# A SwiGLU block: one Silu with a token-major down projection, and gate and val as two 64-row array tiles

## The chip, the cores and the metric

The kernel runs on one core of a Trainium2 chip. The metric is the device time of one execution in microseconds (us), lower is better. PE is TensorE's matrix multiplication, PEld its weight loads, DVE is VectorE, ACT is ScalarE, POOL is GpSimd, SP is SyncE, which here only starts DMAs. "Granted clock" is the share of TensorE's full clock that the hardware let through (1.00 is full).

## The reference, cut to what matters

A depthwise causal convolution with 7 taps runs over the sequence (x is 8 x 4096 x 192, one softmaxed set of taps for each of 8 heads of 24 channels). A gated feed-forward block follows on all 32768 tokens:

```python
g   = x @ w_gate                 # 192 -> 1536
val = x @ w_val                  # 192 -> 1536
out = (g * sigmoid(g) * val) @ w_out     # 1536 -> 192
```

## The kernel before

The tokens are cut into 64 blocks of 512. For a block, x is fetched, transposed on PE so that channels lie on partitions (two halves of 96), and convolved. Taps are shared out: ACT makes the first product and the products for POOL, DVE adds 3 or 4 taps, POOL adds the last 2 or 3. The 1536 hidden features are 12 chunks of 128. This happens for each chunk:

```python
def emit_chunk(j, xcb, hlist):
    gps = ppool.tile([P, TB], fp32, tag="gate", name="gate")   # two buffers each
    for h in range(2):
        nc.tensor.matmul(gps, wg_r[:, h, ts(j, P)], xcb[h], start=(h == 0), stop=(h == 1))
    vps = ppool.tile([P, TB], fp32, tag="val", name="val")
    for h in range(2):
        nc.tensor.matmul(vps, wv_r[:, h, ts(j, P)], xcb[h], start=(h == 0), stop=(h == 1))
    nc.scalar.activation(sj, gps, AF.Sigmoid)
    nc.vector.tensor_tensor(qj, gps, sj, op=ALU.mult)          # q = gate * sigmoid
    if j in A_CHUNKS:                                          # 4 of 12
        nc.vector.tensor_tensor(hj, qj, vps, op=ALU.mult)
    else:                                                      # 8 of 12
        nc.scalar.copy(v_sb, vps)
        nc.gpsimd.tensor_tensor(hj, qj, v_sb, op=ALU.mult)

def emit_f2(j, acc, hlist):              # down projection, features on partitions
    for m in range(2):
        nc.tensor.matmul(acc[:, m, :], wo_r[:, j, m * Dh : (m + 1) * Dh], hlist[j], ...)

def emit_store(b, acc):
    nc.vector.transpose(outB, acc)       # 96 x 1024, back to token rows in 32 x 32 squares
    ...                                  # six DMAs of 128-byte runs
```

The conv of the next block is emitted among the chunks of this one:

```python
for k in DVE_TAPS[h]:
    nc.vector.scalar_tensor_tensor(out=xacc, in0=xcin[:, k : k + TB],
        scalar=wsm[h][:, k : k + 1], in1=xacc, op0=ALU.mult, op1=ALU.add)
... # ACT makes tmp for each k in POOL_TAPS[h]
for i, tmp in enumerate(tmps):           # POOL adds them; the last add gives xc_h
    nc.gpsimd.tensor_tensor(o, xacc, tmp, op=ALU.add)
```

## Time and profile before

| | before |
|---|---|
| time, median of 2 runs | 1695.25 us (1694.97 to 1695.53) |
| a block of 512 tokens, span / 64 | 26.5 us |
| busy share PE, DVE, ACT, POOL | 77, 72, 61, 64% |
| mean granted clock | 0.876 |

Parts 1, 2 and 4 of the page of the kernel before (busy us, share of the span and instructions; the granted clock in tenths, over 40 slices; the chain of waits that ended last):

```profile
PE 1304.3 (77%) x5120; PEld 605.6 (36%) x5120; DVE 1229.0 (72%) x1547; ACT 1040.1 (61%) x1861; POOL 1080.7 (64%) x967
...
PEclk9898888888898898888988888889889889898899
...
POOL 26%; PE 24%; DVE 23%; issue 15%; ACT 9%; POOLq 0%; DVEq 0%; ACTq 0%
```

No engine is full and the chain hops over all of them: the kernel is bound by a loop of hand-overs, not by one engine. Part 5 of the page, the groups of instructions (line, engine, operation, out<-in, shapes, count, then busy us, mean ns of one, then the engine's idle time before them and what ended most of it):

```profile
L185 POOL TENSOR_TENSOR h<-q,vsb 128x512 f16<-128x512 f16 x512 | 624.1, 1225 | 436.6 <-DVE q L178 303.9
L190 PE MATMUL acc<-h,wo_sb 128*96 128x512 f16 x1536 | 503.5, 412 | 322.0 <-POOL h L185 316.9
L178 DVE TENSOR_TENSOR q<-gate,sig 128x512 f16<-128x512 f32 x768 | 513.1, 681 | 189.6 <-ACT sig L176 127.5
L145 DVE SCALAR_TENSOR_TENSOR xacc<-xcin,wn_98,xacc 96x512 f32<-96x512 f16 x256 | 273.5, 1068 | 107.5 <-ACT xacc L143 106.9
L145 DVE SCALAR_TENSOR_TENSOR xacc<-xcin,wn_111,xacc 96x512 f32<-96x512 f16 x192 | 261.6, 1362 | 2.0 <-ACT xacc L143 1.6
L201 DVE STREAM_TRANSPOSE outB<-acc 96x1024 f32<-96x1024 f32 x64 | 79.7, 1245 | 140.3 <-PE acc L190 140.1
```

The POOL product is the slow step of the loop: 1.2 us each, and PE waits 317 us for it. The taps (L145) have two means, 1.07 and 1.36 us, for one shape; the shortest are 0.73 us. Every longer one ran beside POOL: the 42 taps (of 448) during which POOL ran no sum or product took 0.73 to 0.75 us each. Here is POOL in the timeline of the kernel before, at the end of a block (start us, us, engine, line, operation):

```profile
818.82 1.26 POOL L161 TENSOR_TENSOR xc<-xacc,tmp_6_7455 96x512 f16<-96x512 f32 x1
820.04 1.15 POOL L185 TENSOR_TENSOR h<-q,vsb 128x512 f16<-128x512 f16 x1
821.15 1.71 POOL L161 TENSOR_TENSOR xc<-xacc,tmp_6_7518 96x512 f16<-96x512 f32 x1
822.83 1.15 POOL L185 TENSOR_TENSOR h<-q,vsb 128x512 f16<-128x512 f16 x1
```

Conv sums and h products share one queue, so an h that PE waits for stands behind sums that nobody yet needs.

### The profile page before, as it was taken

The numbers are of one execution on the slowest core, as the hardware profiler recorded it, in microseconds if no ns is written. First come the engines' busy times: TensorE is split into PE (matmuls) and PEld (weight loads), VectorE is DVE, ScalarE is ACT, GpSimd is POOL, SyncE is SP. The second block draws the span as 40 slices with busy tenths as digits, with TensorE's granted clock in tenths as the row PEclk, the third lists the DMA queues.
The fourth block names the chain that finished last, engine by engine and source line by source line (L and its number), as shares of the span: only waits on it lengthen the run. The fifth ranks groups of instructions, "written<-read, shape, count | busy, mean of one in ns | idle before, by whom it ended". The sixth has DMA issues, their size and how long they took to land.

```text
span 1696.6 us, 18246 instructions
## 1 busy us (share of the span) xinstructions
PE 1304.3 (77%) x5120; PEld 605.6 (36%) x5120; DVE 1229.0 (72%) x1547; ACT 1040.1 (61%) x1861; POOL 1080.7 (64%) x967
## 2 busy tenths in 40 slices
PE   3777777878787787787787877877877878778777
PEld 1333333333333333343333333433333333334333
DVE  5787677777686786776776867777777768677765
ACT  4766656656566666576666665656666656666545
POOL 4777666576666666766666667567566666675664
PEclk9898888888898898888988888889889889898899
DMA  5111102111111111021110111110211101111101
GB/s 139 29 38 28 38 10 47 35 22 38 19 38 29 28 38 38 10 47 30 27 38 19 38 29 28 38 29 19 47 27 30 38 19 38 28 29 19 18 11 28
DMA packets 238813, 55.06 MB, mean 32 GB/s; under 512 B 204024, under 2 KB 238328, under 8 KB 238712
## 3 DMA queue, kind: packets, MB, share of 16 engines
q1 hardware_dynamic: 238712, 53.90, 15.3%
q8 instruction: 40, 0.66, 0.2%
q14 instruction: 61, 0.50, 0.1%
HBM read 28.71 MB, written 25.17 MB: 32 GB/s over the span
## 4 chain that ended last, share of the span: by engine, by line
POOL 26%; PE 24%; DVE 23%; issue 15%; ACT 9%; POOLq 0%; DVEq 0%; ACTq 0%
POOL h L185 13%; DVE q L178 11%; POOL xc L161 10%; PE gate L167 9%; DVE xacc L145 9%; PE val L172 6%; PE acc L190 6%; ACT sig L176 5%; POOL xacc L161 4%; DVE h L181 3%; ACT vsb L184 2%; ACT xacc L143 0%; ACT xcin L140 0%; DVE outB L201 0%; POOLq L185 0%
## 5 line engine op out<-in xcount | busy, mean ns | idle before, releaser
L185 POOL TENSOR_TENSOR h<-q,vsb 128x512 f16<-128x512 f16 x512 | 624.1, 1225 | 436.6 <-DVE q L178 303.9
L190 PE MATMUL acc<-h,wo_sb 128*96 128x512 f16 x1536 | 503.5, 412 | 322.0 <-POOL h L185 316.9
L176 ACT ACTIVATE sig<-gate 128x512 f16<-128x512 f32 x768 | 456.7, 595 | 476.0 <-PE gate L167 440.7
L178 DVE TENSOR_TENSOR q<-gate,sig 128x512 f16<-128x512 f32 x768 | 513.1, 681 | 189.6 <-ACT sig L176 127.5
L167 PE MATMUL gate<-xc,wg_sb 96*128 96x512 f16 x1536 | 515.6, 420 | 40.6 <-DVE q L178 32.7
L172 PE MATMUL val<-xc,wv_sb 96*128 96x512 f16 x1536 | 537.0, 422 | 1.3 <-ACT vsb L184 0.5
L190 PEld LDWEIGHTS <-wo_sb 128*96 128x96 f16 x1536 | 199.4, 130 | 537.3 <-issue 414.5
L145 DVE SCALAR_TENSOR_TENSOR xacc<-xcin,wn_98,xacc 96x512 f32<-96x512 f16 x256 | 273.5, 1068 | 107.5 <-ACT xacc L143 106.9
L184 ACT CAST vsb<-val 128x512 f16<-128x512 f32 x512 | 297.6, 581 | 39.5 <-PE val L172 38.9
L145 DVE SCALAR_TENSOR_TENSOR xacc<-xcin,wn_111,xacc 96x512 f32<-96x512 f16 x192 | 261.6, 1362 | 2.0 <-ACT xacc L143 1.6
L167 PEld LDWEIGHTS <-wg_sb 96*128 96x128 f16 x1536 | 161.3, 105 | 253.8 <-issue 135.5
L172 PEld LDWEIGHTS <-wv_sb 96*128 96x128 f16 x1536 | 162.5, 106 | 207.0 <-issue 70.1
L201 DVE STREAM_TRANSPOSE outB<-acc 96x1024 f32<-96x1024 f32 x64 | 79.7, 1245 | 140.3 <-PE acc L190 140.1
L181 DVE TENSOR_TENSOR h<-q,val 128x512 f16<-128x512 f16 x256 | 171.8, 671 | 7.9 <-PE val L172 1.2
L143 ACT ACTIVATE xacc<-xcin,wn_98 96x512 f32<-96x512 f16 x64 | 46.2, 722 | 75.4 <-POOL xc L161 75.3
L143 ACT ACTIVATE xacc<-xcin,wn_111 96x512 f32<-96x512 f16 x64 | 46.0, 719 | 34.9 <-POOL xc L161 34.9
L138 POOL COPY xcin<-xcin 96x6 f16<-96x6 f16 x112 | 37.5, 335 | 37.4 <-ACT xcin L140 37.4
L126 PE MATMUL xt_129<-identity,x_sb 128*96 128x128 f32 x4 | 1.1, 421 | 19.9 <-DMA x_sb<-in_x_dram 19.9
L109 POOL CAST wo_sb<-wo_st 128x2304 f16<-128x2304 f32 x1 | 2.1, 2104 | 17.4 <-DMA wo_st<-in_moe_w_out_dram 17.4
L104 DVE CAST wv_sb<-wv_st 96x3072 f16<-96x3072 f32 x1 | 1.8, 1757 | 9.0 <-DMA wv_st<-in_moe_w_val_dram 9.0
L126 PEld LDWEIGHTS xt_129<-identity,x_sb 128*96 128x96 f32 x4 | 0.6, 190 | 19.9 <-issue 19.9
L99 ACT CAST wg_sb<-wg_st 96x3072 f16<-96x3072 f32 x1 | 2.8, 2751 | 4.7 <-DMA wg_st<-in_moe_w_gate_dram 4.7
(1043 smaller groups left out, 963.2 us busy)
## 6 DMA issues: line engine op xcount, KB each, us to landing
x_sb<-in_x_dram SPq DMA_DIRECT2D x64, 384.0 KB, 3.4
out_dram<-outB SPq DMA_DIRECT2D x384, 64.0 KB, 1.9
wg_st<-in_moe_w_gate_dram SPq DMA_DIRECT2D x1, 1152.0 KB, 8.5
wv_st<-in_moe_w_val_dram SPq DMA_DIRECT2D x1, 1152.0 KB, 13.1
wo_st<-in_moe_w_out_dram SPq DMA_DIRECT2D x1, 1152.0 KB, 15.3
wraw_87<-in_weight_dram SPq DMA_DIRECT2D x1, 2.6 KB
wraw_100<-in_weight_dram SPq DMA_DIRECT2D x1, 2.6 KB
```

The costliest lines, as they stand in the source:

```text
L143: nc.scalar.mul(xacc, xcin[:, 0:TB], wsm[h][:, 0:1])
L145: nc.vector.scalar_tensor_tensor(out=xacc, in0=xcin[:, k : k + TB], scalar=wsm[h][:, k : k + 1], in1=xacc, op0=ALU.mult, op1=ALU.add,)
L161: nc.gpsimd.tensor_tensor(o, xacc, tmp, op=ALU.add)
L167: nc.tensor.matmul(gps, wg_r[:, h, ts(j, P)], xcb[h], start=(h == 0), stop=(h == 1))
L172: nc.tensor.matmul(vps, wv_r[:, h, ts(j, P)], xcb[h], start=(h == 0), stop=(h == 1))
L176: nc.scalar.activation(sj, gps, AF.Sigmoid)
L178: nc.vector.tensor_tensor(qj, gps, sj, op=ALU.mult)
L181: nc.vector.tensor_tensor(hj, qj, vps, op=ALU.mult)
L184: nc.scalar.copy(v_sb, vps)
L185: nc.gpsimd.tensor_tensor(hj, qj, v_sb, op=ALU.mult)
L190: nc.tensor.matmul(acc[:, m, :], wo_r[:, j, m * Dh : (m + 1) * Dh], hlist[j], start=(j == 0), stop=(j == NCH - 1),)
L201: nc.vector.transpose(outB, acc)
```

## The change

The intent is threefold. Silu in one ACT instruction removes q, the val copy and POOL's products, so that DVE makes h with one product per chunk. The down projection becomes token-major: h is the stationary operand, so the result comes out with tokens on partitions, and the transpose and small stores go. And gate and val, whose 192 input channels had been two 96-row matmuls each, become three slots of 64 channels: gate on array rows 0 to 63 and val on rows 64 to 127 are meant to run at the same time, so that 4 matmul times become 3. For this the conv result is copied by 8 on-chip DMAs a block into both row ranges. The core of the diff (weight loading, pool lines and signatures cut):

```diff
+    def emit_slots(xcs):
+        xq = cpool.tile([P, NQ, TB], fp16, tag="xq", name="xq")
+        for lo in (0, Q):
+            ...          # 4 copies for each row range, all on the SP queue
+                nc.sync.dma_start(out=xq[r : r + n, c // Q, :],
+                                  in_=xcs[c // Dh][c % Dh : c % Dh + n, :])
+        return xq
     def emit_chunk(j, xcb, hlist):
-        ...              # two gate matmuls, two val matmuls, 96 rows each
+        for q in range(NQ):
+            for lo, ps in ((0, gps), (Q, vps)):
+                nc.tensor.matmul(ps, w_r[lo : lo + Q, q, ts(j, P)],
+                    xcb[lo : lo + Q, q, :], start=(q == 0), stop=(q == NQ - 1))
-        nc.scalar.activation(sj, gps, AF.Sigmoid)
-        nc.vector.tensor_tensor(qj, gps, sj, op=ALU.mult)
-        ...              # h on DVE (4 chunks), or val copy on ACT and h on POOL (8)
+        nc.scalar.activation(sj, gps, AF.Silu)
+        nc.vector.tensor_tensor(hj, sj, vps, op=ALU.mult)
     def emit_f2(j, acc, hlist):
-        for m in range(2):
-            nc.tensor.matmul(acc[:, m, :], wo_r[:, j, m * Dh : (m + 1) * Dh], hlist[j], ...)
+        for s in range(SUBS):
+            nc.tensor.matmul(acc[s // 2][:, s % 2, :], hlist[j][:, ts(s, P)], wo_r[:, j, :], ...)
     def emit_store(b, acc):
-        nc.vector.transpose(outB, acc)       # and six stores
+        nc.scalar.copy(o_sb[:, 0:2, :], acc[0])
+        nc.vector.tensor_copy(o_sb[:, 2:4, :], acc[1])   # and one store
-                if j == 5: ...  elif j == 8: ...     # conv halves of the next block
+                if j == 1: ...  elif j == 4: ...
```

More of the change, by code (lines that the diff above doesn't have):

```diff
@@ L53 @@
     POOL_TAPS = {0: (5, 6), 1: (4, 5, 6)}
-    A_CHUNKS = frozenset((0, 3, 6, 9))
     F2_LAG = 2
+    Q = 64
+    NQ = D // Q
     const_pool = ctx.enter_context(tc.tile_pool(name="const", bufs=1))
@@ L94 @@
         wsm.append(wn)
-    wg_st = wpool.tile([Dh, 2, Dff], fp32, tag="wg_st", name="wg_st")
-    nc.sync.dma_start(out=wg_st, in_=moe_w_gate.rearrange("(h p) f -> p h f", p=Dh))
-    wg_r = wpool.tile([Dh, 2, Dff], fp16, tag="wg_sb", name="wg_sb")
-    nc.scalar.copy(wg_r, wg_st)
-    wv_st = wpool.tile([Dh, 2, Dff], fp32, tag="wv_st", name="wv_st")
-    nc.sync.dma_start(out=wv_st, in_=moe_w_val.rearrange("(h p) f -> p h f", p=Dh))
-    wv_r = wpool.tile([Dh, 2, Dff], fp16, tag="wv_sb", name="wv_sb")
-    nc.vector.tensor_copy(wv_r, wv_st)
+    w_st = wpool.tile([P, NQ, Dff], fp32, tag="w_st", name="w_st")
+    nc.sync.dma_start(out=w_st[0:Q], in_=moe_w_gate.rearrange("(q p) f -> p q f", p=Q))
+    nc.sync.dma_start(out=w_st[Q:P], in_=moe_w_val.rearrange("(q p) f -> p q f", p=Q))
+    w_r = wpool.tile([P, NQ, Dff], fp16, tag="w_sb", name="w_sb")
+    nc.scalar.copy(w_r[:, 0, :], w_st[:, 0, :])
+    nc.vector.tensor_copy(w_r[:, 1, :], w_st[:, 1, :])
+    nc.gpsimd.tensor_copy(w_r[:, 2, :], w_st[:, 2, :])
     wo_st = wpool.tile([P, NCH, D], fp32, tag="wo_st", name="wo_st")
@@ L162, in emit_conv_half @@
         return xc_h
+    def emit_slots(xcs):
+        xq = cpool.tile([P, NQ, TB], fp16, tag="xq", name="xq")
+        for lo in (0, Q):
+            c = 0
+            while c < D:
+                n = min(Q - c % Q, Dh - c % Dh)
+                r = lo + c % Q
+                nc.sync.dma_start(
+                    out=xq[r : r + n, c // Q, :],
+                    in_=xcs[c // Dh][c % Dh : c % Dh + n, :],
+                )
+                c += n
+        return xq
     def emit_chunk(j, xcb, hlist):
@@ L165, in emit_chunk @@
         gps = ppool.tile([P, TB], fp32, tag="gate", name="gate")
-        for h in range(2):
-            nc.tensor.matmul(
-                gps, wg_r[:, h, ts(j, P)], xcb[h], start=(h == 0), stop=(h == 1)
-            )
         vps = ppool.tile([P, TB], fp32, tag="val", name="val")
-        for h in range(2):
-            nc.tensor.matmul(
-                vps, wv_r[:, h, ts(j, P)], xcb[h], start=(h == 0), stop=(h == 1)
-            )
-        sj = hpool.tile([P, TB], fp16, tag="sig", name="sig")
@@ L176, in emit_chunk @@
-        nc.scalar.activation(sj, gps, AF.Sigmoid)
-        qj = hpool.tile([P, TB], fp16, tag="q", name="q")
-        nc.vector.tensor_tensor(qj, gps, sj, op=ALU.mult)
-        hj = hpool.tile([P, TB], fp16, tag="h", name="h", bufs=4)
-        if j in A_CHUNKS:
-            nc.vector.tensor_tensor(hj, qj, vps, op=ALU.mult)
-        else:
-            v_sb = hpool.tile([P, TB], fp16, tag="vsb", name="vsb")
-            nc.scalar.copy(v_sb, vps)
-            nc.gpsimd.tensor_tensor(hj, qj, v_sb, op=ALU.mult)
+        for q in range(NQ):
+            for lo, ps in ((0, gps), (Q, vps)):
+                nc.tensor.matmul(
+                    ps,
+                    w_r[lo : lo + Q, q, ts(j, P)],
+                    xcb[lo : lo + Q, q, :],
+                    start=(q == 0),
+                    stop=(q == NQ - 1),
+                )
@@ L186, in emit_chunk @@
+        sj = hpool.tile([P, TB], fp16, tag="sig", name="sig", bufs=3)
+        nc.scalar.activation(sj, gps, AF.Silu)
+        hj = hpool.tile([P, TB], fp16, tag="h", name="h", bufs=5)
+        nc.vector.tensor_tensor(hj, sj, vps, op=ALU.mult)
         hlist.append(hj)
     def emit_f2(j, acc, hlist):
-        for m in range(2):
+        for s in range(SUBS):
             nc.tensor.matmul(
-                acc[:, m, :],
-                wo_r[:, j, m * Dh : (m + 1) * Dh],
-                hlist[j],
-                start=(j == 0),
+                acc[s // 2][:, s % 2, :],
+                hlist[j][:, ts(s, P)],
+                wo_r[:, j, :],
+                start=(j == 0 and s % 2 == 0),
@@ L195, in emit_f2 @@
                 stop=(j == NCH - 1),
+                skip_group_check=True,
             )
@@ L199, in emit_store @@
         t0 = b * TB
-        outB = opool.tile([Dh, 2, TB], fp32, tag="outB", name="outB")
-        nc.vector.transpose(outB, acc)
-        for m in range(2):
-            for a in range(Dh // 32):
-                dst = bass.AP(
-                    tensor=out.tensor,
-                    offset=t0 * D + m * Dh + 32 * a,
-                    ap=[[D, 32], [32 * D, TB // 32], [1, 32]],
-                )
-                nc.sync.dma_start(out=dst, in_=outB[ts(a, 32), m, :])
+        o_sb = opool.tile([P, SUBS, D], fp32, tag="o_sb", name="o_sb")
+        nc.scalar.copy(o_sb[:, 0:2, :], acc[0])
+        nc.vector.tensor_copy(o_sb[:, 2:4, :], acc[1])
+        nc.sync.dma_start(
+            out=out[t0 : t0 + TB, :].rearrange("(s p) d -> p s d", p=P), in_=o_sb
+        )
     x_sb_next = emit_fetch(0)
@@ L219 @@
         if p == 0:
-            xc_blk[0] = [emit_conv_half(0, h, xts[h]) for h in range(2)]
+            xc_blk[0] = emit_slots([emit_conv_half(0, h, xts[h]) for h in range(2)])
             continue
         b = p - 1
-        acc = apool.tile([Dh, 2, TB], fp32, tag="acc", name="acc")
+        acc = [
+            apool.tile([P, 2, D], fp32, tag=f"acc{i}", name=f"acc{i}") for i in range(2)
+        ]
         hlist = []
@@ L229 @@
             if p < n_blocks:
-                if j == 5:
-                    xc_blk[p] = [emit_conv_half(p, 0, xts[0]), None]
-                elif j == 8:
-                    xc_blk[p][1] = emit_conv_half(p, 1, xts[1])
+                if j == 1:
+                    xc0 = emit_conv_half(p, 0, xts[0])
+                elif j == 4:
+                    xc_blk[p] = emit_slots([xc0, emit_conv_half(p, 1, xts[1])])
         for j in range(NCH - F2_LAG, NCH):
```

## The prediction

> **What bounds it now.** 64 blocks of 512 tokens, about 26.3 us each (span 1696.6 us). No engine is full: the busy table gives PE 77%, DVE 72%, POOL 64%, ACT 61%; the chain that ended last is shared by POOL 26%, PE 24%, DVE 23%, issue 15%. It is a coupled pipeline: matmul, sigmoid, q on DVE, ScalarE copy of val, product on POOL (1225 ns x512), down matmul. Largest waits: sigmoid for gate matmul (440.7 us), down matmul for POOL's h (316.9), POOL's h for q (303.9). In the timeline, from 804 to 817 us the clock is 1.00 and DVE 99% busy; from 817 to 829 us PE waits for POOL (conv sums queue ahead of h) and the clock falls to 0.75.
>
> **What changes, per block (groups' means, timeline).**
> - DVE: 12 q products (0.68 us) go; all 12 h products become SBUF sig x PSUM val, a form that cost 0.67 us. The 1.25 us transpose becomes a half copy[...]. The 7 conv taps stay: 0.65 to 0.74 us alone, up to 2.29 beside POOL (means 1.07, 1.36).[...] About 19 -> 14 us.
> - POOL: 8 h products (9.8 us) go: about 17 -> 7 us, so fewer slow taps.
> - ACT: 8 val copies (0.47 us start to start) go, a half copy comes: about 16 -> 13 us. Silu est. like sigmoid, 0.595.
> - PE: gate+val were 4 matmuls of 0.215 us a chunk; now 3 pairs, 0.65 us if they overlap fully.[...] Down: 2x0.215 becomes 4 matmuls of 192 columns with a new weight load each[...].[...]
> - DMA: 8 on-chip copies; 6 -> 1 stores, in 768 B runs. Est. 2 us to land (old stores: 1.9). With conv emitted at chunks 1 and 4, they land 2 to 3 us before use.
>
> **Critical path after.** The built kernel's queues show two phases a block. A (first 4 or 5 chunks): conv work interleaves with Silu and h; I count 12.7 us from the last block's final gate/val pairs to the fifth h, set by DVE (7 taps, two waiting for POOL's sums) behind the accumulator drain. B (the rest): paced by PE or by the two-buffer loop pair, Silu, product (2.2 us per 2 chunks): 6 x 1.1 to 1.25 us. Sum 19.5 to 20.3 us a block; x64 plus some 25 us start: about 1275 us, 25% less.
>
> **Predicted:** 1275 us, 8 in 10 in 1140 to 1430. Faster by over 2%: 0.95; within 2%: 0.03; slower: 0.02.
>
> **What would show it.**
> - A pair's matmuls start within tens of ns, three pairs take 0.65 us; if not, 1.29.
> - [...]
> - Taps' mean about 0.9 us; POOL 30 to 35% busy, DVE 70%, ACT 65%.
> - Waits: PE for DVE's h at the front of a block; none long for xq DMAs.
> - Clock above 0.9, as PE no longer waits for POOL.
>
> **What would make it wrong.** Pairs serialised: about 24 us a block, 1560.[...] xq landing late: PE stalls and goes cold at block starts, +2 to 4 us. Opposite: phases overlapping better, 17.5 us a block, 1145.

What is cut from it came from no trace of this case, or was an estimate that does not say from what it was made. Its sums came to about 14 us a block on DVE, and to 19.5 to 20.3 us a block on the path (the two phases as written add up to 12.7 + 6.6 to 7.5, that is 19.3 to 20.2), so about 1275 us. Terms of both are cut: the half copy that takes the transpose's place on DVE (measured later: 0.56 us), and what a chunk costs on TensorE with four down matmuls and two changes between 64-row and 128-row matmuls (measured later: 1.19 us). The lower 1.1 us a chunk of phase B is half of the loop's 2.2 us; the upper 1.25 us can't be derived from what is left.

## More of the kernel before

The program order is not the order on the engines: a scheduler builds each engine's queue from readiness and order of emission.

## The result, and the profile after

| | before | after |
|---|---|---|
| time, median | 1695.25 us | 1361.55 us (1361.24 to 1361.87, 2 runs) |
| ratio to before | 1 | 0.803 (95% interval 0.801 to 0.806) |
| a block, span / 64 | 26.5 us | 21.2 us |
| busy share PE, DVE, ACT, POOL | 77, 72, 61, 64% | 84, 70, 59, 35% |
| mean granted clock | 0.876 | 0.919 |

A ratio, here and below, is the mean time of one kernel's fast runs over that of the other's of the same rounds, so it is not quite the ratio of the medians quoted.

Parts 1, 2, 4 and 5 of the page after, to be held against those of before:

```profile
PE 1142.1 (84%) x8192; PEld 498.6 (37%) x8192; DVE 953.4 (70%) x1291; ACT 798.3 (59%) x1413; POOL 478.9 (35%) x456
...
PEclk9999898998998889989989889889899899888899
...
PE 48%; DVE 29%; issue 15%; ACT 7%; DMA 1%; SPq 0%; ACTq 0%; DVEq 0%
...
L185 PE MATMUL val<-xq,w_sb 64*128 64x512 f16 x2304 | 684.5, 412 | 153.0 <-DVE h L195 152.6
L195 DVE TENSOR_TENSOR h<-sig,val 128x512 f16<-128x512 f16 x768 | 523.8, 682 | 314.1 <-ACT sig L193 311.4
L146 DVE SCALAR_TENSOR_TENSOR xacc<-xcin,wn_111,xacc 96x512 f32<-96x512 f16 x192 | 238.2, 1241 | 2.7 <-ACT xacc L144 0.4
L146 DVE SCALAR_TENSOR_TENSOR xacc<-xcin,wn_98,xacc 96x512 f32<-96x512 f16 x256 | 196.4, 767 | 32.3 <-ACT xacc L144 29.9
```

POOL has left the chain. Half 0's taps (wn_98) fell from 1068 to 767 ns, but half 1's (wn_111) are still at 1241, and PE waits 153 us for DVE's h. The timeline of the kernel after, in one block, shows where these two meet:

```profile
805.44 1.26 POOL L162 TENSOR_TENSOR xacc<-xacc,tmp_5_9589 96x512 f32<-96x512 f32 x1 [1.30 <-DVE xacc L146]
805.88 3.05 DVE L146 SCALAR_TENSOR_TENSOR xacc<-xcin,wn_111,xacc 96x512 f32<-96x512 f16 x2
806.78 1.59 POOL L162 TENSOR_TENSOR xc<-xacc,tmp_6_9591 96x512 f16<-96x512 f32 x1
808.85 0.67 DVE L195 TENSOR_TENSOR h<-sig,val 128x512 f16<-128x512 f16 x1
809.58 0.37 PE L185 MATMUL val<-xq,w_sb 64*128 64x512 f16 x1 [2.01 <-DVE h L195]
```

Two half-1 taps are queued in front of the fourth h. They meet half 0's two sums on POOL and take 3.05 us, where the two taps at the start of the same block take 1.53. The first tap begins while the first sum runs (to 806.70), and the pair of taps ends at 808.93, 0.56 us after the second sum (808.37); a tap alone takes 0.75 us. The whole trace agrees: the 311 taps (of 448) beside which no sum ran took 0.73 to 0.75 us each, the other 137 took 1.49 us on average. Why the hardware makes a tap beside a sum longer, no run shows. Meanwhile PE sits idle for 2.01 us, since val has two buffers and the fourth h holds one. The same block by windows (stretch in us, its length, busy us and count for PE, PEld, DVE, ACT, POOL, then granted clock, DMA share, GB/s):

```profile
800.60:807.40 6.80, 6.05 (x45) 2.53 (x44) 6.32 (x10) 6.80 (x14) 2.56 (x4) 1.00 0.42 116
807.40:809.58 2.18, 0.17 (x2) 0.00 (x1) 2.18 (x3) 0.43 (x1) 0.97 (x1) 1.00 0.01 1
809.58:811.10 1.52, 1.52 (x9) 0.63 (x8) 1.45 (x3) 0.60 (x1) 0.77 (x1) 0.71 0.37 94
811.10:813.60 2.50, 2.50 (x13) 0.84 (x14) 0.80 (x2) 0.60 (x1) 2.38 (x4) 0.50 0.10 27
813.60:820.40 6.80, 6.60 (x58) 3.07 (x54) 3.76 (x6) 3.15 (x6) 0.67 (x1) 1.00 0.11 29
```

Soon after the gap the clock falls to half for 3.41 us (810.21 to 813.62 in the trace's clock records), so the loss is the gap and then slow chunks, which follow each other after 1.53, 2.15 and 1.35 us. The chunks after those run at full clock, 1.19 us each. The whole trace repeats this: it has 60 waits of about 2.0 us, and at 59 of them the clock falls to half within 1.6 us of the wait's end.

### The profile page after: what moved, and what is told of

It reads as the page before. It is cut to its first block, busy times and chain, and to the rows that moved or that the text cites. A ratio compares the mean times of both kernels' runs of the same rounds, so it can differ in the third digit from the quotient of the medians.

```text
span 1359.5 us, 22727 instructions
## 1 busy us (share of the span) xinstructions
PE 1142.1 (84%) x8192; PEld 498.6 (37%) x8192; DVE 953.4 (70%) x1291; ACT 798.3 (59%) x1413; POOL 478.9 (35%) x456
## 4 chain that ended last, share of the span: by engine, by line
PE 48%; DVE 29%; issue 15%; ACT 7%; DMA 1%; SPq 0%; ACTq 0%; DVEq 0%
PE gate L185 25%; DVE xacc L146 18%; DVE h L195 11%; PE val L185 6%; ACT xacc L144 3%; ACT sig L193 3%; DMA x_sb<-in_x_dram 1%; ACT o_sb L213 0%; PE acc_446 L201 0%; PE acc_699 L201 0%; PE acc_16118 L201 0%; PE acc_11325 L201 0%; PE acc_14361 L201 0%; PE acc_8289 L201 0%; PE acc_5253 L201 0%
## 5 line engine op out<-in xcount | busy, mean ns | idle before, releaser
L185 PE MATMUL val<-xq,w_sb 64*128 64x512 f16 x2304 | 684.5, 412 | 153.0 <-DVE h L195 152.6
L195 DVE TENSOR_TENSOR h<-sig,val 128x512 f16<-128x512 f16 x768 | 523.8, 682 | 314.1 <-ACT sig L193 311.4
L185 PE MATMUL gate<-xq,w_sb 64*128 64x512 f16 x2304 | 701.2, 410 | 25.0 <-ACT sig L193 17.3
L185 PEld LDWEIGHTS <-w_sb 64*128 64x128 f16 x4608 | 211.8, 97 | 483.9 <-issue 391.2
L201 PEld LDWEIGHTS <-h 128*128 128x128 f16 x3072 | 232.1, 102 | 347.9 <-issue 315.9
L146 DVE SCALAR_TENSOR_TENSOR xacc<-xcin,wn_111,xacc 96x512 f32<-96x512 f16 x192 | 238.2, 1241 | 2.7 <-ACT xacc L144 0.4
L139 POOL COPY xcin<-xcin 96x6 f16<-96x6 f16 x112 | 46.1, 411 | 531.7 <-ACT xcin L141 531.7
L146 DVE SCALAR_TENSOR_TENSOR xacc<-xcin,wn_98,xacc 96x512 f32<-96x512 f16 x256 | 196.4, 767 | 32.3 <-ACT xacc L144 29.9
L127 PE MATMUL xt_128<-identity,x_sb 128*96 128x128 f32 x4 | 1.1, 417 | 20.3 <-DMA x_sb<-in_x_dram 20.3
L127 PEld LDWEIGHTS xt_128<-identity,x_sb 128*96 128x96 f32 x4 | 0.6, 187 | 20.3 <-issue 20.2
L162 POOL TENSOR_TENSOR xacc<-xacc,tmp_5_5794 96x512 f32<-96x512 f32 x1 | 1.3, 1263 | 12.0 <-DVE xacc L146 12.0
L162 POOL TENSOR_TENSOR xacc<-xacc,tmp_5_11866 96x512 f32<-96x512 f32 x1 | 1.3, 1263 | 12.0 <-DVE xacc L146 12.0
L162 POOL TENSOR_TENSOR xacc<-xacc,tmp_5_1746 96x512 f32<-96x512 f32 x1 | 1.3, 1265 | 11.9 <-DVE xacc L146 11.9
L162 POOL TENSOR_TENSOR xacc<-xacc,tmp_5_13890 96x512 f32<-96x512 f32 x1 | 1.3, 1263 | 11.9 <-DVE xacc L146 11.9
L162 POOL TENSOR_TENSOR xacc<-xacc,tmp_5_7818 96x512 f32<-96x512 f32 x1 | 1.3, 1263 | 11.9 <-DVE xacc L146 11.9
L162 POOL TENSOR_TENSOR xacc<-xacc,tmp_5_15912 96x512 f32<-96x512 f32 x1 | 1.3, 1267 | 11.8 <-DVE xacc L146 11.8
## 6 DMA issues: line engine op xcount, KB each, us to landing
wo_st<-in_moe_w_out_dram SPq DMA_DIRECT2D x1, 1152.0 KB, 15.2
```

The lines of the kernel that those rows point to most:

```text
L127: nc.tensor.transpose(xt[:, ts(s, P)], x_sb[:, s, h * Dh : (h + 1) * Dh], identity)
L139: nc.gpsimd.tensor_copy(xcin[:, 0:pad], prev_xcin[h][:, TB : TB + pad])
L185: nc.tensor.matmul(ps, w_r[lo : lo + Q, q, ts(j, P)], xcb[lo : lo + Q, q, :], start=(q == 0), stop=(q == NQ - 1),)
L195: nc.vector.tensor_tensor(hj, sj, vps, op=ALU.mult)
L201: nc.tensor.matmul(acc[s // 2][:, s % 2, :], hlist[j][:, ts(s, P)], wo_r[:, j, :], start=(j == 0 and s % 2 == 0), stop=(j == NCH - 1), ski ...
```

## The experiments

Twelve kernels ran, three rounds each, on chips where the kernel before took 1694 to 1695 us. All gave the right result except the one that was wrong on purpose. The theory after reading the two traces was: work taken off DVE and POOL gave the gain; the tiles gave little; a collision of taps with POOL sums, and the clock after it, held the rest back. The rivals were that TensorE's new form carries the gain, and that DVE's sum of work paces the block whatever its order.

### One part undone at a time

**a_half96: row tiles and on-chip copies undone, the rest kept.**

```diff
-        for q in range(NQ):
-            for lo, ps in ((0, gps), (Q, vps)):
-                nc.tensor.matmul(ps, w_r[lo : lo + Q, q, ts(j, P)], ...)
+        for w, ps in ((wg_r, gps), (wv_r, vps)):
+            for h in range(2):
+                nc.tensor.matmul(ps, w[:, h, ts(j, P)], xcb[h], ...)
```

> Changed kernel with only the row tiles and the on-chip copies undone: gate and val as four 96-row matmuls from the two conv halves, as before. Theory (row tiling is worth little here): a chunk on TensorE costs 4 x 0.215 + 0.35 us = 1.21 us without the two gaps of about 0.09 us at mode changes, against 1.19 us measured with tiles; so 1361 us within 30 us. Rival (the pairs are the gain): +0.215 us per chunk on the path, 12 x 64 x 0.215 = +165 us, about 1525 us.

Measured: 1090.95 us, ratio 0.644 (0.643 to 0.645), clock 0.993. Both expectations missed: it is 20% faster than the whole change. The TensorE part of the theory held, though. PE in the timeline of a_half96, one chunk when nothing holds it up:

```profile
705.49 0.60 PE L176 MATMUL gate<-xc,wg_sb 96*128 96x512 f16 x2
705.92 0.59 PE L176 MATMUL val<-xc,wv_sb 96*128 96x512 f16 x2
706.35 0.49 PE L188 MATMUL acc<-wo_sb,h 128*128 128x192 f16 x4
706.68 0.60 PE L176 MATMUL gate<-xc,wg_sb 96*128 96x512 f16 x2
```

and in the kernel after:

```profile
836.49 0.39 PE L185 MATMUL gate<-xq,w_sb 64*128 64x512 f16 x1
836.49 0.39 PE L185 MATMUL val<-xq,w_sb 64*128 64x512 f16 x1
...
836.93 0.38 PE L185 MATMUL gate<-xq,w_sb 64*128 64x512 f16 x1
836.94 0.38 PE L185 MATMUL val<-xq,w_sb 64*128 64x512 f16 x1
837.24 0.34 PE L201 MATMUL acc_9807<-wo_sb,h 128*128 128x192 f16 x2
...
837.68 0.39 PE L185 MATMUL gate<-xq,w_sb 64*128 64x512 f16 x1
```

Both repeat after 1.19 us (706.68 - 705.49, and 837.68 - 836.49). With tiles the pairs do start together, and take three matmul times of 0.215 us instead of four (two 96-row matmuls take 0.43 us, 705.49 to 705.92 above). But from the last pair to the first down matmul is 0.31 us, 0.095 more than a matmul time, and from there to the next gate is 0.44 us, where the same four down matmuls took 0.33 us without tiles. Those 0.095 + 0.11 us eat the 0.215 saved. The two gaps stand where 64-row and 128-row matmuls meet (the "mode changes" of the expectation), and where 96-row and 128-row matmuls meet in the run without tiles there are none. What fills them is not told apart here: without tiles the first weight load of the down matmuls starts 0.21 us before its matmul (706.14 and 706.35 in the trace), with tiles it starts together with it (837.24), and a load takes 0.10 us (102 ns on average for those of the down matmuls).

Equal chunks don't explain 270 us. The built kernels differ in something else: without tiles, the scheduler put DVE's taps in another order (mostly one by one between the products). So this run alone can't say whether the tiles or the order cost the time; the crossing below does.

**b_featdown: the token-major down projection undone.**

```diff
-        for s in range(SUBS):
-            nc.tensor.matmul(acc[s // 2][:, s % 2, :], hlist[j][:, ts(s, P)], wo_r[:, j, :], ...)
+        for m in range(2):
+            nc.tensor.matmul(acc[:, m, :], wo_r[:, j, m * Dh : (m + 1) * Dh], hlist[j], ...)
```

(with the old transpose and stores)

> Changed kernel with only the token-major down projection undone (feature-major accumulator, 1.25 us stream transpose, 6 stores). Theory: down goes from 4 x 0.088 = 0.35 to 2 x 0.215 = 0.43 us in the 7 chunks paced by TensorE (+0.6 us), and the drain at the block boundary goes from about 0.5 to 1.25 us (+0.75): +1.35 us x 64, about 1450 us. Rival (the form of the down projection is off the path): 1361 us within 20.

Measured: 1353.33 us, ratio 0.799 (0.798 to 0.800), clock 0.979. It fits the rival, but it decides little: here too the scheduler changed DVE's order (every other block has the half-1 taps split up), so that a dearer form may be offset by a better order. Inconclusive. Its trace shows something else, though: PE waits 1.83 us for an h in one block and 1.03 us in the next. The clock fell to half after 14 of the 29 waits of 1.83 us, and after one of the 30 of 1.03 us.

**d_sigmoid: Silu undone.**

```diff
-        nc.scalar.activation(sj, gps, AF.Silu)
-        nc.vector.tensor_tensor(hj, sj, vps, op=ALU.mult)
+        nc.scalar.activation(sj, gps, AF.Sigmoid)
+        nc.vector.tensor_tensor(qj, gps, sj, op=ALU.mult)
+        ...      # h on DVE for chunks 0, 3, 6, 9; else val copy on ACT, h on POOL
```

> Changed kernel with only the Silu undone: Sigmoid, q on VectorE, the val copy on ScalarE and h on GpSimd for 8 of 12 chunks come back. Theory (most of the gain is the work taken off VectorE and GpSimd): 1600 to 1720 us, near the kernel before, though TensorE has tiles and the token-major form. Rival (TensorE changes carry the gain): about 1450 us.

Measured: 1700.75 us, ratio 1.004 (1.003 to 1.006). The theory holds: without Silu, tiles and the token-major form together give nothing, in the order that was built.

**l_silu: the kernel before with Silu alone.**

```diff
-        nc.scalar.activation(sj, gps, AF.Sigmoid)
-        nc.vector.tensor_tensor(qj, gps, sj, op=ALU.mult)
-        ...      # the two ways to h
+        nc.scalar.activation(sj, gps, AF.Silu)
+        nc.vector.tensor_tensor(hj, sj, vps, op=ALU.mult)
```

> Kernel before with one part of the change alone: Silu on ScalarE and all h products on VectorE; matmuls, down projection, transpose and stores as before. Theory (work taken off VectorE and GpSimd is the gain; TensorE then costs 6 x 0.215 = 1.29 us a chunk): 1091 + 64 x (1.2 + 0.75) = about 1215 us, in 1150 to 1300, faster than the whole change. Rival (the other two parts are needed too): above 1361 us.

Measured: 1108.91 us, ratio 0.655 (0.654 to 0.656), clock 0.999. This part without the other two is 253 us faster than the whole change. (sig and h have the buffers of the change, 3 and 5. Here too the scheduler built another order on DVE, with half 1's taps spread, so this is Silu together with the order that came with it.) It beat the expectation too, which had added TensorE's extra time to a run that was not wholly bound by TensorE. Parts 1 and 4 of the page of l_silu:

```profile
PE 1069.6 (97%) x5120; PEld 546.8 (49%) x5120; DVE 903.5 (82%) x1291; ACT 757.0 (68%) x1349; POOL 453.0 (41%) x455
...
PE 95%; DVE 1%; ACT 1%; issue 0%; POOL 0%; POOLq 0%; DVEq 0%
```

This is what the change could have looked like: the loop of hand-overs is gone, the chain is PE from end to end, and the clock stays up. With TensorE as the bound, the form of the down projection counts too: a chunk repeats after 1.30 us here and after 1.19 us in a_half96, which differ on TensorE in that form.

### The collision and the clock

**e_nosum0: POOL's two sums of half 0 taken away (wrong result).** DVE and ACT do the same work in the same order; DVE's last tap writes the conv result itself.

```diff
-                out=xacc,
+                out=xc_h if (h == 0 and k == DVE_TAPS[h][-1]) else xacc,
...
-        for i, tmp in enumerate(tmps):
+        for i, tmp in enumerate(tmps if h == 1 else []):
             nc.gpsimd.tensor_tensor(o, xacc, tmp, op=ALU.add)
```

> Changed kernel with GpSimd's two conv sums of half 0 taken away (result wrong on purpose); VectorE and ScalarE do the same work. These sums are what two VectorE taps of half 1 wait behind (3.05 us for two taps that alone take 1.4). Theory: the collision costs 1.65 us a block itself and, through the 2 us gap on TensorE that it makes, a cold clock for the next two chunks (2.14 us instead of 1.19): about 3.3 us a block, 1150 us. Rival 1 (the collision only, clock apart): 1361 - 64 x 1.65 = 1255 us. Rival 2 (hidden behind other work): above 1320 us.

Measured: 1173.81 us, ratio 0.693 (0.692 to 0.694), clock 0.993, relative error 0.53. That is 188 us less than the whole change, 2.9 us a block; both simple rivals fall, and the theory's 1150 us was 24 us too low. The sums that two taps met cost the collision and its aftermath.

**f_fill: six dummy matmuls into the gap.** They write chunk 5's gate bank before the real matmuls overwrite it.

```diff
+        if j == 5:
+            for _ in range(6):
+                nc.tensor.matmul(gps, w_r[0:Q, 0, ts(j, P)], xcb[0:Q, 0, :], start=True, stop=True)
```

> Changed kernel plus six dummy matmuls (1.3 us) into chunk 5's gate bank, overwritten by the real ones, placed where TensorE waits about 2 us for VectorE's fourth product; result stays right. Theory (that gap lowers the clock afterwards): granted clock rises from 0.92 to about 0.98, and chunks 5 and 6 go from 2.14 to 1.19 us: 1240 to 1290 us. Rival (the gap isn't what lowers the clock, or the slow chunks are hidden): 1361 to 1400 us.

Measured: 1277.35 us, ratio 0.754 (0.753 to 0.755), clock 0.997, DVE in the same steady order as in the changed kernel. More work on TensorE made it 84 us faster. PE in the timeline of f_fill, from chunk 5's val on:

```profile
707.60 0.37 PE L190 MATMUL val<-xq,w_sb 64*128 64x512 f16 x1 [0.72 <-DVE h L200]
...
708.77 0.39 PE L190 MATMUL gate<-xq,w_sb 64*128 64x512 f16 x1
...
710.03 0.39 PE L190 MATMUL gate<-xq,w_sb 64*128 64x512 f16 x1
```

The collision is still there (PE still waits 0.72 us for that h), but the chunks after it take 1.17 and 1.26 us instead of the 1.72 and 2.15 of a block in the changed kernel. After none of the 61 waits of this size does the clock fall. So here it is the gap that lowers the clock, and the clock costs 84 us. The collision itself, 3.05 - 1.53 = 1.52 us for 64 blocks, is 97 us; 97 + 84 = 181, next to the 188 that e_nosum0 gave back.

**g_late: only the order of DVE changed.** Half 1's taps come after the fourth, fifth and sixth product.

```diff
-        for k in DVE_TAPS[h]:
-            nc.vector.scalar_tensor_tensor(out=xacc, ...)
+        for i, k in enumerate(DVE_TAPS[h]):
+            with tc.issue_after(after[i]) if i < len(after) else nullcontext():   # order only
+                nc.vector.scalar_tensor_tensor(out=xacc, ...)
```

> Changed kernel with only an order on VectorE: the three taps of half 1 come after the 4th, 5th and 6th product (one each) instead of two before the 4th and one after; same arithmetic. Theory: the taps no longer meet half 0's sums on GpSimd, the 4th product comes 2 us earlier, TensorE stays warm: 17 to 18 us a block, 1110 to 1170 us; the on-chip copies may now land just as needed. Rival (VectorE's sum of work paces the block, order doesn't matter): above 1320 us.

Measured: 1181.07 us, ratio 0.697 (0.696 to 0.698), clock 0.998. It lands 11 us above the stated band, and far from the rival: the same arithmetic with three DVE instructions moved is 180 us faster. DVE in the timeline of g_late, at the fourth and fifth h:

```profile
705.28 0.69 DVE L197 TENSOR_TENSOR h<-sig,val 128x512 f16<-128x512 f16 x1 [0.81 <-PE gate L187]
705.89 1.22 DVE L148 SCALAR_TENSOR_TENSOR xacc<-xcin,wn,xacc 96x512 f32<-96x512 f16 x1
707.03 0.67 DVE L197 TENSOR_TENSOR h<-sig,val 128x512 f16<-128x512 f16 x1
707.63 0.74 DVE L148 SCALAR_TENSOR_TENSOR xacc<-xcin,wn,xacc 96x512 f32<-96x512 f16 x1
```

One tap still meets the end of a sum (1.22 us), but no h that PE needs stands behind two of them.

**g_lateswap: as g_late, with POOL's three sums given to half 0 and two to half 1.**

```diff
-    DVE_TAPS = {0: (1, 2, 3, 4), 1: (1, 2, 3)}
-    POOL_TAPS = {0: (5, 6), 1: (4, 5, 6)}
+    DVE_TAPS = {1: (1, 2, 3, 4), 0: (1, 2, 3)}
+    POOL_TAPS = {1: (5, 6), 0: (4, 5, 6)}
```

> As g_late, and GpSimd's three sums go to half 0, two to half 1 (VectorE three and four taps), so the last conv result of a block is out one sum (1.26 us) earlier. Theory: if in g_late TensorE waits for the on-chip copies at the block start, this takes 0.5 to 1.3 us a block off it (30 to 80 us); if not, equal to g_late within 15 us or a little slower, as half 1 has a fourth tap.

Measured: 1191.72 us, ratio 0.704 (0.703 to 0.705). No gain, so the on-chip copies were not late; g_late's waits agree, with 9.8 us of PE waiting for these copies in the whole run (gate matmuls 7.6, val 2.2).

**h_serial: three gate matmuls, then three val.**

```diff
-        for q in range(NQ):
-            for lo, ps in ((0, gps), (Q, vps)):
+        for lo, ps in ((0, gps), (Q, vps)):
+            for q in range(NQ):
```

> Changed kernel with the six gate and val matmuls of a chunk in another order: three gate, then three val, so neighbours share rows of the array except at one place. Theory (two row tiles overlap only when neighbours in the queue use different rows): the six take 5 x 0.215 = 1.08 us instead of 0.65, +0.43 us in at least 7 chunks a block, 1550 us or more. Rival (TensorE looks ahead and overlaps them in any order): 1361 us within 20.

Measured: 1245.50 us, ratio 0.735 (0.734 to 0.736), clock 0.998. Neither number came, for two reasons. The scheduler again chose another DVE order, the likely reason that it is faster than the whole change (no run shows this apart). And TensorE overlapped the two groups all the same. The built queue has three gates, then three vals, but PE in the timeline of h_serial reads:

```profile
712.01 0.39 PE L185 MATMUL gate<-xq,w_sb 64*128 64x512 f16 x1
712.02 0.39 PE L185 MATMUL val<-xq,w_sb 64*128 64x512 f16 x1
712.23 0.38 PE L185 MATMUL gate<-xq,w_sb 64*128 64x512 f16 x1
712.24 0.38 PE L185 MATMUL val<-xq,w_sb 64*128 64x512 f16 x1
...
712.77 0.50 PE L201 MATMUL acc<-wo_sb,h 128*128 128x192 f16 x4
713.20 0.39 PE L185 MATMUL gate<-xq,w_sb 64*128 64x512 f16 x1
```

Val's first matmul starts 0.01 us after gate's first, though two more gate matmuls stand between them in the queue (of starts alone, as ends are modelled). This chunk, which nothing holds up, repeats after 1.19 us (713.20 - 712.01), as with alternating pairs, and not after the 1.62 us of the expectation. So the rival's overlap is what was measured: here neighbours in the queue need not alternate. How TensorE comes to it, no run shows.

### Tiles crossed with order

In three kernels without tiles the order on DVE, ACT and PE was pinned with order-only edges. Apart from start-up, the first two have the DVE and ACT queues of the changed kernel and of g_late.

```diff
+    SPEC = "c0 O m0 u0 t0 t0 P0 S0 h0 u0 c1 t0 P1 S1 h1 m1 t0 s0 P2 S2 h2 F0 u1 u1 t1 t1 P3 S3 h3 F1 ..."
+    # c copy of x, m first product, u product for POOL, t tap on DVE, s sums on POOL (0 or 1: the half);
+    # P gate and val matmuls, S Silu, h product, F down matmuls of a chunk; O output copies
```

**k_half96_after: the changed kernel's order** (two taps, `t1 t1`, before `h3`).

> No row tiles (four 96-row matmuls a chunk, no on-chip copies), but the order of work on VectorE, ScalarE and TensorE is pinned to the changed kernel's order (two taps of half 1 before the fourth product). Theory A (in the run without tiles it was the scheduler's other order that gave 1091 us; tiles themselves are neutral): 1361 us within 50. Theory B (tiles and their copies cost the time): 1120 us or less. In between: both.

Measured: 1342.68 us, ratio 0.792 (0.791 to 0.794), clock 0.915. Its trace shows the same picture without any row tile: two taps of 3.05 us, a 2.19 us wait of PE behind them, and slow matmuls afterwards (two gate matmuls in 0.86 us, 720.79 to 721.65, where they take 0.43 before the wait). DVE and PE in its timeline:

```profile
714.39 3.05 DVE L147 SCALAR_TENSOR_TENSOR xacc<-xcin,wn,xacc 96x512 f32<-96x512 f16 x2
718.09 0.59 PE L147 MATMUL val<-xc,wv_sb 96*128 96x512 f16 x2 [2.19 <-DVE h L147]
```

**k_half96_late: g_late's order** (`h3 t1 h4 t1 h5 t1`).

> No row tiles, order on all three engines pinned to that of g_late (taps of half 1 after the 4th, 5th, 6th product), which with tiles took 1181 us. Theory A (tiles neutral: 1.19 us a chunk in both forms): 1181 us within 25. Theory B (tiles cost): below 1120 us.

Measured: 1151.72 us, ratio 0.680 (0.679 to 0.681), clock 0.999. The four together:

| order of the queues | with tiles | without tiles |
|---|---|---|
| as in the changed kernel | 1361.55 us | 1342.68 us |
| half 1's taps later (g_late) | 1181.07 us | 1151.72 us |

Down a column, order is worth about 180 to 190 us; along a row, the tiles cost 19 and 29 us. (g_late had only its taps pinned, so 29 us may hold a little of TensorE's order.) Theory A holds for the order: it was not the tiles that held back the change, but the order that the scheduler happened to build around them. "Neutral" was a little too kind to the tiles, though: k_half96_late came out 4 us below theory A's band (1156 to 1206), if well above theory B's 1120.

**k_half96_spread: one tap after each of the first products** (`t0 h0 t0 h1 t0 h2 t0 h3 h4 t1 h5 t1 h6 t1`), conv products of ACT spread likewise.

> No row tiles, pinned order with one tap after each of the first products and half 1's taps after the 5th, 6th and 7th, ScalarE's conv work likewise one a chunk. If TensorE's 12 x 1.19 + 0.86 us a block is then the bound: about 16 us a block, 1030 to 1070 us, below the 1091 us of the free order without tiles. If the drain of the accumulators at the block boundary still paces: 1090 us or more.

Measured: 1048.77 us (1048.60 to 1049.19, 4 runs), ratio 0.619 (0.618 to 0.620), clock 0.999. It beats both kernels, by 38% and 23% of their times. Parts 1 and 4 of its page:

```profile
PE 1008.3 (96%) x6656; PEld 603.7 (58%) x6656; DVE 850.2 (81%) x1291; ACT 794.7 (76%) x1413; POOL 451.5 (43%) x455
...
PE 78%; ACT 8%; DVE 5%; issue 5%; POOL 2%; DMA 2%; SPq 0%; ACTq 0%
```

An estimate from the traces: 12 chunks of 1.19 us (as in a_half96) and 8 transposes of about 0.11 us (four in 0.43 us, 712.52 to 712.95 in this run's trace), 15.2 us a block or 970 us, plus some 30 us of start (the changed kernel's first gate matmul begins at 31.6 us), some 1000 us together, is about what this form needs on TensorE alone.

## Why the prediction was right or wrong

The time (1361.55) lies in the range (1140 to 1430), 87 us above the point (1275). Point by point:

- **What bounds it before: right.** A coupled loop with POOL's product as its slow step. d_sigmoid shows that with that loop kept, the other two parts give nothing; l_silu shows that breaking it is enough, in the order that was built.
- **DVE 19 to 14, ACT 16 to 13, POOL 17 to 7 us: right.** After: 953.4, 798.3 and 478.9 us busy, divided by 64: 14.9, 12.5 and 7.5. Silu cost 594 ns, as sigmoid had (595). (ACT was 59% busy, not the 65% of the list.)
- **Pairs overlap, 0.65 us for three: right.** Two matmuls of a pair start within 0.01 us when nothing delays one of them, and the pairs follow each other after 0.215 us (836.49, 836.72, 836.93 in the trace).
- **A chunk on TensorE: its estimate is cut, so there is nothing to score.** Measured: the down matmuls start 0.083 us apart without tiles, so that the four take 0.33 us where the old form took 0.43, about 0.1 us of TensorE's time less a chunk; the gaps where 64-row and 128-row matmuls meet come to 0.095 and 0.11. The chunk cost 1.19 us. What the prediction did not ask is what the chunk would cost without tiles: also 1.19. So three matmul times in place of four brought nothing here.
- **Copies land in time: right.** 7.6 us of waiting for them in the run.
- **Phase A, "I count 12.7 us from the last block's final gate/val pairs to the fifth h, set by DVE (7 taps, two waiting for POOL's sums)": right, a little short.** In one block the final pairs start at 818.18 and the fifth product ends near 831.45, 13.3 us later, and the two waiting taps are there.
- **Phase B, "6 x 1.1 to 1.25 us": the sum came, but not in the way that was said.** From the end of the fifth product to chunk 11's pairs (838.87) is 7.4 us, inside the 6.6 to 7.5. But the six chunks do not run at 1.1 to 1.25 us. They start at chunk 5's val (830.24), 1.2 us before that end, and take 1.72, 2.15 and four times 1.19, 8.63 us, where six times 1.19 is 7.14. The term mis-sized is the clock: the prediction said "Clock above 0.9, as PE no longer waits for POOL", and 0.919 is above 0.9; but it had the wait for h at the front of a block in its own list and did not charge it with a slow clock afterwards. That costs this block 1.49 us, and f_fill, which takes most of it away, wins 84 us. That it was hidden in phase B's sum by the overlap with phase A is luck.
- **Where the 87 us lie.** The point of 1275 stands for 19.5 us a block, (1275 - 25) / 64, and the block above has 20.7: 0.6 us more in each phase, some 74 us in 64. The rest, some 12 us, is start and end (37 us, not 25). Why phase A is 0.6 us longer than counted was not asked. f_fill, without the slow clock, runs in 1277 us; that this is so near to 1275 is chance.
- **"Taps' mean about 0.9 us": near.** (256 x 767 + 192 x 1241) / 448 = 970 ns, the two halves far apart.
- **What it missed altogether** is the size of what was left to gain. It found the collision while counting, took it as given, and did not see that it came from the built order and could be moved: 180 us.

## What to carry to other kernels

When a change gives less than the work it removes, compare the built queues of the engines before you blame a part of it: here moving three instructions on one engine was worth 180 us, while one part of the change was worth nothing and another alone, with the order that came with it, gave more than the whole. Undoing one part under a free scheduler also changes the order, so pin the order when you ask what a part is worth. And look whether a wait on TensorE costs twice, once for itself and once for a slow clock after it: here waits of 2.0 us did so nearly always (59 of 60), of 1.83 us in half of the cases (14 of 29), of 1.03 us once in 30, of 0.7 us never (61 waits), and filling the gap of 2 us with useless matmuls won 84 us.
